# Twelve in place of eight weight pairs of a second feed-forward layer by seven products

## The chip, the cores and the metric

The kernel runs on one core of a Trainium2 chip. The metric is the device time of one execution in microseconds (us). Engines are called as in the profile: PE (TensorE matmul), PEld (its weight loads), DVE (VectorE), ACT (ScalarE), POOL (GpSimd), SP (SyncE, which issues all DMAs here).

## What is computed

```python
x = A_x                                   # 1 x 2048 x 576
xn = _layernorm(x, axis=-1)
return x + _A_ref(xn, A_wqkv, A_wo) + _B_ref(xn, B_w1, B_b1, B_w2)
# _A_ref: q, k, v = xn @ wqkv, 32 heads of 18; each position attends to 8 positions
#         (itself and every second one before it); softmax; o @ wo
# _B_ref: h = xn @ w1 + b1 (4608 wide); act = h * tanh(softplus(h)); act @ w2
```

All arithmetic is float32.

## The kernel before

**Float32 by halves.** A float32 operand is split into a high part (a cast, on ACT) and a low part (a difference, on DVE or POOL). One product is then three matmuls: high by high, low by high, high by low. A group of six matmuls over two contraction tiles of 128 fills one PSUM bank, and DVE adds that bank to an accumulator in SBUF (an eviction).

**Two halves, 18 pairs.** The 2048 tokens are two halves (`hf` 0 and 1) of 1024, each of two blocks `b` of 512. The 4608 hidden columns are 36 tiles of 128, taken as `NP = 18` pairs `q`. For each half: projections q/k/v (`qkv_item`, in the second half partly `z_part`), then `quad(hf, q)` for each pair, and at the end the output projection (`wo_part`). Within a pair, `m1_part` 0 to 5 computes both tiles of the first layer for both blocks with seven block products instead of eight (sums `Ss` of the activations, differences t0 and t1 of the weights).

**The second layer.** Ordinarily (`m2_pair` in half 0, `m2_cols` in half 1) one pair is four chunks (two blocks by two token groups), each of four banks of six matmuls 128x128 by 128x288. For pairs 0 to 7 of the second half the seven-product scheme is used: two pairs (`qq` 0 and 1) are one group `e`, whose seven items (`p_item`, products `P7, P4, P1, P5, P2, P6, P3`) have 24 matmuls each. The left factors are the activations `A11, A12, A22` and combinations `S1` to `S4` of them (`u_sum`; cast in `u_high`, low part in `u_low`); they are held in float32 until then, in buffers that `raw_act` hands out. The right factors are `B11, B21, B22` of the second layer's weight and the differences `T1` to `T4`. Each product has accumulators of its own, which POOL joins after the last group (`p_join`). Pair `2 * OC` is kept in float32 too and split afterwards (`a_split`). `OC` is the number of groups.

**The weights in DRAM.** Half 0 loads each weight, splits it (`make`), uses it and stores the split form (`keep`); half 1 loads that (`fetch`, `p_fetch`). For the pairs that go by seven products, half 0 also forms T1 to T4 (`t_sum`, `t_high`, `t_low`, `t_keep`, in the pool of tiles `xn`, five buffers) and stores each factor by itself. The second half reads pair `q + 1`'s weights as its pair `q` (`Q1`), so the pairs prepared in half 0 are 1 to `2 * OC`. Likewise differences of the q/k/v weights for `z_part` are prepared in half 0 (`z_load`, `z_sum`, `z_high`, `z_low`, `z_keep`, tiles from `xn`, for `k` = 0 and 1), and the output projection's in half 1 (`wo_load`, `wo_sum`, `wo_keep_high`, `wo_keep_low`, `wo_keep`; read back by `wo_fetch`).

**Order of the work.** Everything is written into a list `plan` of places. Each place holds one TensorE part (a projection item, an `m1_part`, a chunk or a product item); `before(i, fn)` puts side work ahead of place `i`. `spot(hf, q, i)` is place `i` of a pair. Each engine, and the SP queue, executes its own instructions strictly in that order. An ordinary pair has ten places (six parts and four chunks); an odd pair by seven products has nine (parts 0, 1, 2, item, 3, item, 4, item, 5), an even one ten (0, 1, item, 2, item, ...).

**Attention** is a generator (`attention(hf)`) of 73 steps a half, nine for two head groups: four of products q times k (POOL) with a reduction (DVE) one step later, one with the softmax's maximum, one with its sum and the first product with v, three more of those. The steps are dealt out over the plan: each place has a duration in plan units, multiplied by the `rate` of its stretch (`marks`), and the sum is divided into 146 equal shares.

```python
k = next(k for k in range(k + 1, len(plan)) if T[k + 1] > t and ok[k])
```

In half 0 only places 0, 3, 7 and 9 of a pair may take a step (`ok`); in half 1 the pairs by seven products may take them at all places.

Of the kernel before, what the change touches and what calls it, by code (L numbers as in the profile page):

```python
# [14 lines left out]
S, D, F = 2048, 576, 4608  # L15
# [11 lines left out]
NP = NF // 2  # L27
# [3 lines left out]
CU = 2 * DH  # L31
OC = 4
Q1 = [*range(1, NP), 0]
# [6 lines left out]
def block_kernel(ctx: ExitStack, tc: tile.TileContext, x, wq, wo, w1, b1, w2, mask, out):  # L40
# [1292 lines left out]
    def spot(hf, q, i):  # L1333
        return at["s", hf, q, i]

    for q in range(NP):
        if q == 0:
            i = at["q", 0, 3, 1, 0]
            ps_ = dict(raw=i - 3, sums=i - 1, wa=i, wc=i + 1, t0=i + 2, t1=i + 4)
        elif q == 1:  # L1340
            i = at["q", 0, 3, 0, 0]
# [16 lines left out]
    for q in range(1, 2 * OC + 1):  # L1358
        i = spot(0, q, (3,2)[q > 1])
# [12 lines left out]
    for name, k, d in (("T2", 0, 0), ("T2", 1, 1), ("T3", 0, 2), ("B11", 0, 3), ("B11", 1, 4), ("B21", 0, 5),  # L1372
                       ("B21", 1, 6), ("R2", 0, 7), ("T3", 1, 8), ("R3", 0, 9), ("T1", 0, 10), ("T1", 1, 10),
                       ("T4", 0, 11), ("T4", 1, 11), ("B22", 0, 11), ("B22", 1, 11)):
        before(i + d, lambda name=name, k=k: z_fetch(name, k))
    i = spot(0, 9, 4)
    for k in range(2):
        for n, steps in enumerate((
# [4 lines left out]
            for kind, name in steps:  # L1383
                f = dict(l=z_load, s=z_sum, h=z_high, o=z_low, k=z_keep)[kind]
                d = 30 + 2 * n if k else 2 * n if n < 10 else (19, 20, 22, 23, 25, 26, 27)[n - 10]
                before(i + d, lambda f=f, name=name, k=k: f(name, k))
# [64 lines left out]
    before(i + 6, var1)  # L1451
    i = spot(0, NP - 2, 0)
    for jj in range(JB):
# [23 lines left out]
    for q in range(2 * OC + 2):  # L1477
        for i in range(spot(1, q, 0), spot(1, q, 9) + 1):
# [3 lines left out]
             spot(1, 2, 0), spot(1, 2 * OC + 2, 0), spot(1, NP - 1, 0), at["o", 0, 0], at["o", 2, 0]]  # L1482
    rate = (1.15, 0.4, 0.5, 0.8, 1.15, 1.3, 1.2, 0.8, 1.5, 0.8, 0)
    T = [0.0]
# [17 lines left out]

    i = spot(1, *(11,3))
    for k in range(4):
        before(i - 8 + 2 * k, lambda k=k: wo_load(k))
    for n in range(4):
        before(i + (0,2,4,6)[n], lambda n=n: wo_sum(n))
    for n, name in enumerate(("T3", "T1", "T2", "T4", "B11", "B21", "B22", "R", "D")):
        k = i + 10 + (0,5,10,15,20,25,30,35,40)[n]
        if name == "R":  # L1510
            before(k - 8, lambda: wo_rest(0))
        before(k, lambda name=name, n=n: wo_keep_high(name, n))
        before(k + 1, lambda name=name: wo_keep_low(name))
        before(k + 2, lambda name=name: wo_keep(name))
# [69 lines left out]
```

## Time and profile before

| | us |
|---|---|
| median of 3 runs (lowest to highest) | 1123.72 (1123.23 to 1124.98) |
| span of the profiled execution | 1121.6 |
| PE busy | 1109.5 (99%) |
| DVE, POOL, ACT busy | 829.0, 787.7, 492.1 |
| DMA queue, share of 16 engines | 69.2% |

The profiled execution is shown by its span alone, from its first to its last instruction; no time of its own beyond that is given. Busy times of different engines overlap. The granted TensorE clock is 1.000 throughout. Which pair a time belongs to is read from the chain of work in order of time: an ordinary pair takes 24.1 us, pair 17 of the first half begins at 503.85, pair 2 of the second half at 652.96.

### The profile page before, as it was taken

The numbers are of one execution on the slowest core, as the hardware profiler recorded it, in microseconds if no ns is written. First come the engines' busy times: TensorE is split into PE (matmuls) and PEld (weight loads), VectorE is DVE, ScalarE is ACT, GpSimd is POOL, SyncE is SP. The second block draws the span as 40 slices with busy tenths as digits, with TensorE's granted clock in tenths as the row PEclk, the third lists the DMA queues.
The fourth block names the chain that finished last, engine by engine and source line by source line (L and its number), as shares of the span: only waits on it lengthen the run. The fifth ranks groups of instructions, "written<-read, shape, count | busy, mean of one in ns | idle before, by whom it ended". The sixth has DMA issues, their size and how long they took to land.

```text
span 1121.6 us, 18415 instructions
## 1 busy us (share of the span) xinstructions
PE 1109.5 (99%) x6630; PEld 1023.0 (91%) x6630; DVE 829.0 (74%) x1351; ACT 492.1 (44%) x892; POOL 787.7 (70%) x639
## 2 busy tenths in 40 slices
PE   8999999999999999999999999999999999999998
PEld 7999899999999999899999889999999999999998
DVE  6368788888888888877655456687866677776876
ACT  5544645544554545455233355343433343443332
POOL 2488767767689687676788476665789878668632
PEclk9999999999999999999999999999999999999999
DMA  6899885868767849666596797655655477676463
GB/s 200 283 312 318 290 283 205 289 228 284 261 240 258 282 163 345 222 240 214 191 342 238 231 373 249 241 200 174 227 198 189 168 263 269 215 253 248 157 222 104
DMA packets 147487, 271.08 MB, mean 242 GB/s; under 512 B 30114, under 2 KB 86724, under 8 KB 147396
## 3 DMA queue, kind: packets, MB, share of 16 engines
q1 hardware_dynamic: 147396, 269.91, 69.2%
q8 instruction: 52, 0.85, 0.3%
q14 instruction: 39, 0.32, 0.1%
HBM read 160.39 MB, written 109.48 MB: 241 GB/s over the span
## 4 chain that ended last, share of the span: by engine, by line
PE 89%; DVE 4%; POOL 3%; DMA 2%; issue 1%; ACT 1%; DVEq 0%; POOLq 0%; SPq 0%
PE h L657 28%; PE po L755 19%; PE pq L349 11%; PE po L868 10%; PE po L847 7%; PE h L663 5%; PE o L1056 4%; PE z L447 2%; DMA acc<-in_x 1%; POOL accP L856 1%; DVE u L801 1%; POOL pr L534 0%; DVE accP L871 0%; POOL act L709 0%; DMA z_B<-kept_wq 0%
## 5 line engine op out<-in xcount | busy, mean ns | idle before, releaser
L755 PEld LDWEIGHTS po<-w,act 128*128 128x128 f32 x1728 | 236.4, 188 | 7.5 <-DVE acc L759 1.7
L755 PE MATMUL po<-w,act 128*128 128x288 f32 x1728 | 240.8, 295 | 1.4 <-DVE acc L759 1.2
L534 POOL TENSOR_TENSOR pr<-q,kv 128x576 f32<-128x576 f32 x128 | 195.7, 1553 | 18.7 <-DMA q<-q_d 16.9
L572 POOL TENSOR_TENSOR pv<-L,kv 128x576 f32<-128x576 f32 x128 | 174.3, 1461 | 38.7 <-DVE L L565 20.9
L709 POOL TENSOR_TENSOR act<-c,act 128x512 fp32r<-128x512 f32 x81 | 107.1, 1322 | 128.4 <-ACT act L708 125.5
L759 DVE TENSOR_TENSOR acc<-po,acc 128x288 f32<-128x288 f32 x288 | 120.4, 450 | 31.6 <-PE po L755 30.2
L349 PE MATMUL pq<-wq,xt 128*128 128x432 f32 x672 | 136.2, 361 | 1.8 <-ACT xt L83 1.8
L868 PEld LDWEIGHTS po<-w,act 128*128 128x128 f32 x960 | 131.1, 188 | 3.7 <-DVE accP L871 0.4
L868 PE MATMUL po<-w,act 128*128 128x288 f32 x960 | 133.8, 295 | 0.2
L349 PEld LDWEIGHTS pq<-wq,xt 128*128 128x128 f32 x672 | 125.0, 188 | 8.7 <-ACT xt L83 2.7
L703 ACT ACTIVATE c<-c,b1c 128x512 f32<-128x512 f32 x81 | 58.7, 724 | 132.9 <-DVE c L702 132.6
L657 PE MATMUL h<-xt,t 128*128 128x512 f32 x432 | 110.6, 391 | 0.9 <-DVE c L702 0.8
L657 PE MATMUL h<-S,t 128*128 128x512 f32 x432 | 110.4, 391 | 0.0
L691 ACT COPY c<-h 128x512 f32<-128x512 f32 x81 | 47.4, 586 | 136.5 <-PE h L663 78.3
L578 DVE TENSOR_REDUCE og<-pv 128x144 f32<-128x1152 f32 x64 | 85.9, 1343 | 25.4 <-POOL pv L572 25.4
L657 PE MATMUL h<-xt,wa 128*128 128x512 f32 x432 | 104.0, 390 | 0.0
L657 PEld LDWEIGHTS h<-xt,wa 128*128 128x128 f32 x432 | 80.9, 188 | 16.9
L871 DVE TENSOR_TENSOR accP<-po,accP 128x288 f32<-128x288 f32 x160 | 69.6, 454 | 36.1 <-PE po L868 34.5
L847 PEld LDWEIGHTS po<-pw,u 128*128 128x128 f32 x672 | 92.4, 188 | 2.9 <-DVE u L801 0.5
L847 PE MATMUL po<-pw,u 128*128 128x288 f32 x672 | 94.2, 296 | 0.3 <-DVE u L801 0.3
L539 DVE TENSOR_REDUCE L<-pr 128x64 f32<-128x1152 f32 x64 | 85.8, 1341 | 11.2 <-POOL pr L534 11.1
L657 PEld LDWEIGHTS h<-xt,t 128*128 128x128 f32 x432 | 79.0, 188 | 16.1 <-DVE c L702 1.1
(231 smaller groups left out, 1840.5 us busy)
## 6 DMA issues: line engine op xcount, KB each, us to landing
kv<-kv_d SPq DMA_DIRECT2D x64, 396.0 KB, 5.2
kept_t<-t SPq DMA_DIRECT2D x36, 512.0 KB, 5.3
t<-kept_t SPq DMA_DIRECT2D x36, 512.0 KB, 5.4
rw<-in_w SPq DMA_DIRECT2D x36, 320.0 KB, 4.6
kept_wa<-wa SPq DMA_DIRECT2D x18, 640.0 KB, 3.5
kept_w<-w SPq DMA_DIRECT2D x20, 576.0 KB, 4.8
wa<-kept_wa SPq DMA_DIRECT2D x18, 640.0 KB, 6.1
w<-kept_w SPq DMA_DIRECT2D x20, 576.0 KB, 4.5
```

The source lines that it names most:

```text
L349: nc.tensor.matmul(pq[:, 0:432], XT[:, xi, tok], wt[wi][:, hl, 0:432], start=i == 0, stop=i == len(seq) - 1)
L534: nc.gpsimd.tensor_tensor(out=pr[:, x:x + hh], in0=q[:, j0 + x:j0 + x + hh, None, :].to_broadcast([P, hh, W, CU]), in1=win(kt, 0, CU, j0 + ...
L539: nc.vector.tensor_reduce(L[:, k, j0:j0 + hj].rearrange("p j w h -> p (j w h)"), pr.rearrange("p j w (h d) -> p (j w h) d", h=2), axis=AX, ...
L572: nc.gpsimd.tensor_tensor(out=pr[:, x:x + hj].rearrange("p j d w -> p j w d"), in0=L[:, k, x:x + hj, :, h:h + 1].to_broadcast([P, hj, W, DH]),
L578: nc.vector.tensor_reduce(og[:, :, c0:c0 + DH], pr, axis=AX, op=ALU.add)
L657: nc.tensor.matmul(ph, wt[:, wl, wk * P:(wk + 1) * P], X[:, xs, :], start=first and i == 0, stop=last and i == len(seq) - 1, skip_group_ch ...
L709: nc.gpsimd.tensor_tensor(out=a[:, 1, :], in0=t, in1=a[:, 0, :].bitcast(F32), op=ALU.subtract)
L755: nc.tensor.matmul(po, acts[hf, q, b, j][:, al, tok], done["w2", hf, 2 * q + j][:, wl, c * HC:(c + 1) * HC], start=i == 0, stop=i == 5)
L759: nc.vector.tensor_tensor(out=t, in0=po, in1=t, op=ALU.add)
L847: nc.tensor.matmul(po, units[e, k, qq][:, al, tok], w[:, qq, wl, :], start=i == 0, stop=i == 5)
L868: nc.tensor.matmul(po, acts[hf, q, b, j][:, al, tok], done["w2", hf, 2 * q + j][:, wl, c * HC:(c + 1) * HC], start=i == 0, stop=i == 5)
L871: nc.vector.tensor_tensor(out=t, in0=po, in1=t, op=ALU.add)
```

## The change

`OC` becomes 6: the second half's pairs 0 to 11 go by seven products, and the first half prepares T1 to T4 for pairs 1 to 12. The q/k/v differences begin in pair 12 at place 7 instead of pair 9 at place 4, one entry of their list a place. The loads of the second half's x for its layer norm in pair 16 begin two places later. Three of the eleven attention rates differ. The output weights' preparation begins at place 6 of pair 14 (was place 3 of pair 11), in another order and three places apart.

```diff
-OC = 4
+OC = 6
...
-    i = spot(0, 9, 4)
+    i = spot(0, 2 * OC, 7)
     for k in range(2):
         for n, steps in enumerate((
                 [("l", "B12"), ("l", "B22"), ("l", "B11")], [], [("s", "T3")], [("h", "T3")], [("o", "T3"), ("s", "T1")], [],
...
-                d = 30 + 2 * n if k else 2 * n if n < 10 else (19, 20, 22, 23, 25, 26, 27)[n - 10]
+                d = n + 19 * k
                 before(i + d, lambda f=f, name=name, k=k: f(name, k))
...
-    i = spot(0, NP - 2, 0)
+    i = spot(0, NP - 2, 2)
     for jj in range(JB):
         before(i + 2 * jj, lambda jj=jj: x_load(jj))
         before(i + 2 * jj + 6, lambda jj=jj: norm1(jj))
...
     marks = [at["q", 0, 2, 0, 1], at["q", 0, 3, 0, 0], spot(0, 1, 0), spot(0, 2 * OC + 1, 0), at["q", 1, 0, 0, 0], at["z", 0, 0], spot(1, 0, 0),
              spot(1, 2, 0), spot(1, 2 * OC + 2, 0), spot(1, NP - 1, 0), at["o", 0, 0], at["o", 2, 0]]
-    rate = (1.15, 0.4, 0.5, 0.8, 1.15, 1.3, 1.2, 0.8, 1.5, 0.8, 0)
+    rate = (1.15, 0.4, 0.55, 0.8, 1.15, 1.3, 1.2, 0.9, 1.3, 0.8, 0)
...
-    i = spot(1, *(11,3))
+    i = spot(1, 2 * OC + 2, 6)
     for k in range(4):
         before(i - 8 + 2 * k, lambda k=k: wo_load(k))
     for n in range(4):
         before(i + (0,2,4,6)[n], lambda n=n: wo_sum(n))
-    for n, name in enumerate(("T3", "T1", "T2", "T4", "B11", "B21", "B22", "R", "D")):
-        k = i + 10 + (0,5,10,15,20,25,30,35,40)[n]
+    for n, name in enumerate(("T3", "B11", "T2", "B21", "R", "T1", "T4", "B22", "D")):
+        k = i + 7 + 3 * n
         if name == "R":
             before(k - 8, lambda: wo_rest(0))
```

## The prediction

> **What bounds the kernel now.** I read the page first: busy shares and the chain that ended last.
>
> ```profile
> span 1121.6 us, 18415 instructions
> PE 1109.5 (99%) x6630; PEld 1023.0 (91%) x6630; DVE 829.0 (74%) x1351; ACT 492.1 (44%) x892; POOL 787.7 (70%) x639
> PE 89%; DVE 4%; POOL 3%; DMA 2%; issue 1%; ACT 1%; DVEq 0%; POOLq 0%; SPq 0%
> ```
>
> TensorE is busy in all but 12 us of 1121.6, and 89% of the chain is its matmuls. Next the view of waits, TensorE alone, for where it stood:
>
> ```profile
> PE pq L349 <- ACT xt L83: 1.8, 2, 1.1
> PE warm L67 <- POOL ident masks.py:199: 1.3, 1, 1.3
> PE o L1056 <- DVE y L1060: 1.3, 2, 0.7
> PE po L755 <- DVE acc L759: 1.2, 1, 1.2
> PE ta L77 <- ACT xn L182: 0.9, 1, 0.9
> PE h L657 <- DVE c L702: 0.8, 1, 0.8
> PE h L657 <- ACT rt L691: 0.7, 1, 0.7
> PE po L847 <- DVE u L801: 0.3, 1, 0.3
> ```
>
> Apart from the start (1.8 + 1.3 + 0.9) there are four places: 1.3 in the output stage, 1.2 in pair 15 of the first half, 0.8 in its pair 1, and 0.7 and 0.3 in the second half. So a matmul that is dropped comes off the span, unless a queue that was just in time becomes late. Then the windows by stage (columns: window and length, busy time of PE, PEld, DVE, ACT, POOL with instruction counts, clock, DMA share, GB/s), and two pieces of the chain in order of time:
>
> ```profile
> 333.53:357.61 24.08, 24.08 (x147) 22.09 (x147) 21.01 (x31) 11.17 (x20) 22.20 (x18) 1.00 0.62 207
> 607.77:631.80 24.03, 24.03 (x119) 22.49 (x120) 14.04 (x26) 5.66 (x18) 13.69 (x11) 1.00 0.31 92
> 677.77:722.95 45.18, 45.18 (x269) 41.10 (x269) 32.99 (x49) 18.09 (x32) 35.10 (x25) 1.00 0.66 229
> 722.95:768.71 45.76, 45.47 (x270) 41.15 (x269) 35.04 (x57) 19.88 (x31) 27.52 (x20) 1.00 0.61 207
> 848.00:896.27 48.27, 48.27 (x293) 44.19 (x293) 33.50 (x56) 16.09 (x24) 43.76 (x35) 1.00 0.57 207
> ```
>
> ```profile
> 683.67 3.17 PE po L847 x24
> 852.54 3.18 PE po L868 x24
> ```
>
> Two pairs by seven products take 45.18 us, two ordinary ones 48.27; both are all TensorE. One item or one chunk, 24 matmuls, takes 3.17 us (132.1 ns a matmul).
>
> **The change, part by part.** The sum is made against the profiled execution, span 1121.6; the median of the runs, 1123.72, is 2.1 above it, and I carry the difference over unchanged.
>
> *Matmuls.* Two more groups of two pairs: 2 x (8 chunks - 7 items) = 2 chunks less, 2 x 3.17 = **-6.34**. The two windows above say the same: 48.27 - 45.18 = 3.09 each. The Trainium skill, "TensorE: Matmul & The Clock Gate", section "Back-to-back issue gap", gives N / 2.4 + 2.5 ns for a warm matmul, for N = 288 an estimate of 122.5 ns; the gain by it would be 48 x 122.5 = 5.88 us. The row's 132.1 ns decides, and the page would make the forecast 0.46 us later.
>
> *Side work in the first half, pairs 9 to 12* (now like pairs 1 to 8), and in the second:
>
> ```profile
> L303 POOL TENSOR_TENSOR twT<-rw,twT 128x288 f32<-128x288 f32 x16 | 15.9, 997 | 1.3
> L313 DVE TENSOR_TENSOR twT<-twT,twhT 128x576 fp32r<-128x576 f32 x16 | 13.8, 894 | 0.3
> L308 ACT CAST twhT<-twT 128x576 fp32r<-128x576 f32 x16 | 10.8, 676 | 15.3 <-POOL twT L303 15.3
> L801 POOL TENSOR_TENSOR u<-ra,u 128x512 fp32r<-128x512 f32 x14 | 18.9, 1354 | 4.7 <-ACT u L795 4.5
> L801 DVE TENSOR_TENSOR u<-rm,u 128x512 fp32r<-128x512 f32 x12 | 11.8, 981 | 3.6 <-ACT u L795 3.6
> L795 ACT CAST u<-ra 128x512 fp32r<-128x512 f32 x22 | 13.5, 619 | 17.1 <-DVE ra L789 8.4 <-PE po L847 6.9 <-POOL ra L789 1.8
> L539 DVE TENSOR_REDUCE L<-pr 128x64 f32<-128x1152 f32 x64 | 85.8, 1341 | 11.2 <-POOL pr L534 11.1
> kept_w<-w SPq DMA_DIRECT2D x20, 576.0 KB, 4.8
> kept_T<-twhT SPq DMA_DIRECT2D x16, 288.0 KB, 4.8
> ```
>
> Per first-half pair: POOL 3 differences (3 x 0.997 = 3.0), DVE one difference and two low parts (taken at 1.0 too, + 2 x 0.894 = 2.8), ACT 2 x 0.676 = 1.4. SP issues 7 stores of 288 KB where it had 2 of 576: 864 KB more. Per second-half group: 14 unit casts for 8 (ACT +6 x 0.619 = 3.7), 14 low parts for 8 and 8 combinations, less 4 evictions: about +11 on DVE and POOL together; SP loads 7 x 576 KB for 4 x 576, three issues more. Cover: pairs 1 to 8 and groups 0 to 3 do just this now, and TensorE loses 0.8 + 0.3 us in all of them. I cost it at nothing by itself; without the cover the upper bound is the whole 2.8 of DVE a pair, 11.2 us. The SP queue has some 20 issues more in a stretch of 96 us; q/k/v differences used to be loaded and stored there and now come later.
>
> *Attention.* Its 146 steps are dealt out by plan time times `rate`. Worked through with the new OC and rates, the total falls from 894.1 to 821.2 plan units, so the steps move: first-half pairs 1 to 8 have 19 steps (were 15), 9 to 12 have 9 (were 13), 13 to 16 have 14 (were 12). In the second half pairs 2 to 13 have 45 (were 45), but pairs 0 and 1 have 7 of that half's own (were 2), and what is left after pair 17 is 2 steps (was 6). That last shift matters in the output stage, where these two reductions stood ahead of the evictions that TensorE waited for:
>
> ```profile
> 1056.52 1.34 DVE L578 TENSOR_REDUCE og<-pv 128x144 f32<-128x1152 f32 x1
> 1059.90 1.34 DVE L578 TENSOR_REDUCE og<-pv 128x144 f32<-128x1152 f32 x1
> ```
>
> Now the last step stands before the second of the four final chunks: **-1.3** (bounds -1.3 and 0). The first second-half steps load their k and q five plan places earlier, into the stretch with a DMA share of 0.31 (window 607.77), and no TensorE wait above is for them: 0.
>
> *The stall in pair 15.* A softmax step was followed in the next place by a value step, so DVE stood 2.40 us for POOL and its evictions came late:
>
> ```profile
> 458.56 1.35 DVE L578 TENSOR_REDUCE og<-pv 128x144 f32<-128x1152 f32 x1 [2.40 <-POOL pv L572]
> 463.90 1.54 DVE L759 TENSOR_TENSOR acc<-po,acc 128x288 f32<-128x288 f32 x4
> ```
>
> In the new plan these two steps are two places apart (14.7 and 14.9): **-1.2**. What comes in its place: the q/k/v differences, one list entry a place instead of every second, run from pair 12 place 7 to pair 16 place 2, beside 3 or 4 attention steps a pair. Pair 10 (window 333.53, 4 steps and the same differences at half the density) had POOL at 22.20 of 24.08 and no TensorE idle. One more difference of POOL a pair, 1 to 1.4 us, brings the four-step pairs 13 and 15 to some 23.5: full. Their loads also wait in the SP queue for tiles of the last stores of pair 12 (one landing, 4.8). Bounds 0 and 4 x 1.25; I take **+0.8**, nearer pair 10, which passed clean.
>
> *More steps in pairs 1 to 8.* In pair 1 a value step comes in at place 3, just ahead of the DVE chain behind the 0.8 wait; its reduction is 1.34, of which the chain has about 0.5 to spare (the idle time in the first row below): **+0.9** (0 to 1.34). In pair 3 the softmax step comes to place 3, with its reduction, 1.34, and what the three rows of such a step show:
>
> ```profile
> 126.56 0.69 DVE L257 TENSOR_TENSOR t<-tt,t 128x512 fp32r<-128x512 f32 x1 [0.51 <-ACT t L256]
> 188.91 1.00 DVE L549 TENSOR_TENSOR L<-L,mk 2x256 f32<-2x256 f32 x1
> 189.95 0.42 DVE L553 TENSOR_REDUCE m<-L 128x32 f32<-128x256 f32 x1
> 190.40 0.43 DVE L555 TENSOR_TENSOR L<-L,m 128x256 f32<-128x256 f32 x1
> ```
>
> 3.2 us together, ahead of four evictions: 0 to 3.2. I take **+0.8**, nearer the lower end, since in pairs 2 to 8 such steps pass now without a TensorE wait, though at places with less beside them.
>
> *Products of the second half.* An item writes four banks; evictions must be done before the next item comes round. At the first item of an odd pair they are nearly late:
>
> ```profile
> 728.80 1.36 DVE L801 TENSOR_TENSOR u<-ra_r,u 128x512 fp32r<-128x512 f32 x1 [1.82 <-ACT u L795]
> 730.08 1.77 DVE L789 TENSOR_TENSOR ra<-ra,ra_r 128x512 f32<-128x512 f32 x1
> 731.78 1.34 DVE L539 TENSOR_REDUCE L<-pr 128x64 f32<-128x1152 f32 x1
> 733.04 1.54 DVE L853 TENSOR_TENSOR accP<-po,accP 128x288 f32<-128x288 f32 x4
> 733.72 3.38 PE L847 MATMUL po<-pw,u 128*128 128x288 f32 x24
> ```
>
> The first of the four evictions ends near 733.49, and TensorE writes again at 733.72: a margin of about 0.2. Seven steps a group come where there were six (ten in the last, for eight), over six groups instead of four; at pair 11 place 3 it is a softmax step, 0.85 more than the plain reduction, so 0.6 late. Against 0.3 lost before, I take **+1.2** more (0 to 14 new items x 0.3 = 4.2).
>
> *Preparation of the output weights.* Four loads, four POOL sums and nine cast/low/store steps move from pair 11 to pairs 14 to 17, three places apart instead of five. Ordinary pairs there have DVE 33.5 of 48.27. Between the last one's store and the products that read it lie four chunks, 4 x 3.17 = 12.7 us: a store and a load of 4.8 each fit. SP holds its reload behind its store, and the attention loads behind that are few by then: 0, at most +1.
>
> Sum: -6.34 - 1.3 - 1.2 + 0.8 + 0.9 + 0.8 + 1.2 = -5.1. Profiled span 1116.5; time 1123.72 - 5.1 = **1118.6**.
>
> **Rivals.**
>
> *Nothing new stalls.* Every cover holds: -6.34 - 1.3 - 1.2 - 0.3 = -9.1, **1114.6**. For it: pairs 2 to 8 lost nothing. Against: the 0.2 margin.
>
> *Given back in pairs 13 to 16.* POOL is full, DVE waits for it in order as at 458.56, and each of the four pairs loses the 1.25 that pair 15 lost: +5.0 for the +0.8, **1122.8**. For it: POOL 22.20 with half the density. Against: that window's PE is 24.08 of 24.08. The Trainium skill, "SBUF — State Buffer", section "Who interferes with whom", has a DVE instruction with two SBUF inputs and a GpSimd one that reads SBUF exclude each other for a whole instruction, which speaks against the change, since nearly all that it adds is of these two kinds. The trace agrees in that L789 takes 1.77 at 730.08; it has no row in which this cost TensorE more than the waits above.
>
> *Slower.* In the products of the second half DVE is late as a rule: with the 0.2 margin gone, each item that gets one more reduction of 1.34 ahead of its evictions costs 1.1 us of TensorE. Without the term taken above the time is 1117.4; slower than 1125.97 needs 8 of the 42 items. At 12 it is 1117.4 + 13.2 = **1130.6**. Against: DVE is busy 35.04 of 45.76 with six steps, and one more adds 1.5.
>
> *The change doesn't drop the matmuls* can't be: their number follows from OC.
>
> **How the numbers follow.** About 0.2% (2.2 us) is what a measurement can tell: faster is below 1121.5, slower above 1126.0. Forecast 0.73, its own range 1115.5 to 1121.0; nothing new stalls 0.10; given back 0.12; slower 0.05. Faster 0.73 + 0.10 + 0.02 of the given-back case = 0.85; same 0.10; slower 0.05. The range 1115.2 to 1122.5 leaves out slower (0.05), most of the stall-free case (0.07) and half of given back (0.06).
>
> **What would show it.** L847 with 1008 matmuls for 672 and L868 with 576 for 960; two more two-pair windows near 45.2. No TensorE wait on L1060 early in the output stage and none in pair 15 at places 4 to 6; new ones on L702 in pair 1, L759 in pair 3 and in pairs 13 to 16, on L801 or L853 among the products. Wrong it would be if a wait names a DMA (the SP queue's part undercosted), or if the PE waits grow past 14 us in all.

## The result, and the profile after

| | before | after |
|---|---|---|
| median of 4 runs (lowest to highest), us | 1123.47 (1122.92 to 1124.98) | 1156.53 (1153.18 to 1160.01) |
| ratio | | 1.029 [1.0268, 1.0312] |
| span of the profiled execution | 1121.6 | 1158.2 |

Forecast was 1118.6, with a range up to 1122.5. The kernel became 33 us slower instead of 5 faster. The profiled execution of the changed kernel is the slowest of its four, so what is read from its trace adds up to 36.6 us. The page of the changed kernel: span, busy times, the clock in 40 slices, the chain by engine.

```profile
span 1158.2 us, 18408 instructions
PE 1119.3 (97%) x6582; PEld 1025.2 (89%) x6582; DVE 859.8 (74%) x1379; ACT 502.3 (43%) x913; POOL 812.4 (70%) x655
PEclk9999999999999999899998999999999998999999
PE 74%; POOL 11%; DVE 6%; issue 4%; ACT 2%; DMA 1%; SPq 0%; POOLq 0%; DVEq 0%; ACTq 0%
```

The 48 matmuls are gone (6582 for 6630), yet PE is busy 9.8 us longer. Span less PE busy is 38.9 us for 12.1. The busy shares of DVE and POOL did not rise at all: 74 and 70% before and after. Who TensorE waited for (total, times, longest):

```profile
PE h L657 <- DVE c L702: 7.8, 4, 3.8
PE h L657 <- DVE rt L702: 5.6, 3, 3.2
PE z L447 <- ACT zqs L456: 4.8, 2, 4.3
PE po L755 <- DVE acc L759: 4.5, 1, 4.5
PE po L847 <- DVE accP L853: 2.1, 2, 1.5
```

These twelve waits are 24.8 us: single stalls, not a broad slowing. The five longest in the timeline of TensorE (start, duration; in brackets the idle time before and its releaser):

```profile
131.82 2.86 PE L657 MATMUL h<-xt,t 128*128 128x512 f32 x6 [2.07 <-DVE c L702]
478.49 1.81 PE L755 MATMUL po<-w,act 128*128 128x288 f32 x6 [4.51 <-DVE acc L759]
621.20 2.53 PE L447 MATMUL z<-zraw_T,S 128*128 128x432 f32 x6 [4.33 <-ACT zqs L456]
769.02 1.94 PE L657 MATMUL h<-xt,t 128*128 128x512 f32 x6 [3.15 <-DVE rt L702]
969.68 2.93 PE L657 MATMUL h<-xt,t 128*128 128x512 f32 x6 [3.82 <-DVE c L702]
```

Six matmuls of L657 take 1.52 us otherwise; here 2.86 and 2.93 in two of the rows. Behind each of the five the granted clock fell to half. Windows over those stretches (window, length, busy PE, PEld, DVE, ACT, POOL, clock, DMA share, GB/s):

```profile
131.92:135.33 3.41, 3.41 (x8) 2.65 (x9) 3.41 (x6) 2.31 (x4) 2.86 (x3) 0.50 0.77 228
476.67:483.50 6.83, 5.01 (x21) 5.01 (x22) 5.03 (x10) 2.32 (x4) 3.94 (x4) 0.50 0.57 206
620.03:626.86 6.83, 5.66 (x16) 5.21 (x17) 3.33 (x7) 2.40 (x8) 3.88 (x4) 0.50 0.03 10
770.21:773.63 3.42, 3.42 (x13) 2.79 (x12) 3.42 (x4) 0.03 (x1) 3.31 (x3) 0.50 0.20 43
968.19:975.02 6.83, 5.33 (x16) 4.57 (x17) 4.76 (x11) 3.76 (x5) 3.29 (x4) 0.50 0.14 49
```

In these 27.3 us PE was busy 22.83, which full speed would have done in half: 11.4 us lost. The account against before is idle time +26.8, half clock +11.4, matmuls -6.3: 31.9 of the 36.6 us between the spans; the other 4.7 are in PE's busy time and are not assigned.

By stages, from the first matmul of a pair in each trace (after minus before): +5.8 at the start of pair 13 of the first half, +11.3 at pair 17, +21.5 at pair 2 of the second half, +33.3 at pair 8, +37.9 at pair 14, +38.3 at pair 17, +36.6 at the end. So the loss is 5.8 in pairs 1 to 12, 5.5 in 13 to 16 (all in 15), 10.2 in the q/k/v stage, 11.8 in pairs 2 to 7, 4.6 net in pairs 8 to 13, 0.4 in 14 to 16, and -1.7 at the end.

The 11.8 us of pairs 2 to 7 are mainly seven waits, 8.9 us together, and one half-clock window (1.7). Ahead of the longest of the waits (769.02 above) stand these two instructions of DVE:

```profile
767.03 1.34 DVE L539 TENSOR_REDUCE L<-pr 128x64 f32<-128x1152 f32 x1
768.29 0.68 DVE L702 TENSOR_TENSOR rt<-h,rt 128x512 f32<-128x512 f32 x1
```

The reduction of an attention step stands right ahead of the addition L702 that TensorE waits for. Before, at the same point of the work, it stood four us earlier (731.78, L702 at 735.69) and no wait followed.

### The profile page after: what moved, and what is told of

The parts are those of the page before. It is cut to its first block, busy times and chain, and to the rows that moved or that the text cites. A ratio compares the mean times of both kernels' runs of the same rounds, so it can differ in the third digit from the quotient of the medians.

```text
span 1158.2 us, 18408 instructions
## 1 busy us (share of the span) xinstructions
PE 1119.3 (97%) x6582; PEld 1025.2 (89%) x6582; DVE 859.8 (74%) x1379; ACT 502.3 (43%) x913; POOL 812.4 (70%) x655
## 4 chain that ended last, share of the span: by engine, by line
PE 74%; POOL 11%; DVE 6%; issue 4%; ACT 2%; DMA 1%; SPq 0%; POOLq 0%; DVEq 0%; ACTq 0%
PE h L657 23%; PE po L755 16%; PE po L847 9%; PE pq L349 8%; PE po L868 5%; PE o L1056 5%; PE h L663 4%; POOL pv L572 3%; PE z L447 2%; POOL pr L534 2%; POOL act L709 2%; POOL s L608 1%; DVE L L539 1%; POOL twT L303 1%; DVE w L257 1%
## 5 line engine op out<-in xcount | busy, mean ns | idle before, releaser
L755 PEld LDWEIGHTS po<-w,act 128*128 128x128 f32 x1728 | 238.8, 190 | 11.5 <-DVE acc L759 5.4
L755 PE MATMUL po<-w,act 128*128 128x288 f32 x1728 | 243.4, 297 | 4.7 <-DVE acc L759 4.5
L534 POOL TENSOR_TENSOR pr<-q,kv 128x576 f32<-128x576 f32 x128 | 199.8, 1586 | 21.0 <-DMA q<-q_d 21.0
L709 POOL TENSOR_TENSOR act<-c,act 128x512 fp32r<-128x512 f32 x69 | 92.4, 1339 | 106.0 <-ACT act L708 101.9
L847 PEld LDWEIGHTS po<-pw,u 128*128 128x128 f32 x1008 | 138.9, 189 | 10.8 <-DVE accP L853 3.4
L847 PE MATMUL po<-pw,u 128*128 128x288 f32 x1008 | 143.0, 297 | 4.4 <-DVE accP L853 2.1
L657 PE MATMUL h<-xt,t 128*128 128x512 f32 x432 | 114.2, 400 | 13.5 <-DVE c L702 7.8
L657 PE MATMUL h<-S,t 128*128 128x512 f32 x432 | 110.7, 391 | 0.7 <-ACT c L691 0.4
L578 DVE TENSOR_REDUCE og<-pv 128x144 f32<-128x1152 f32 x64 | 86.0, 1343 | 30.9 <-POOL pv L572 25.6
L657 PEld LDWEIGHTS h<-xt,t 128*128 128x128 f32 x432 | 80.4, 191 | 30.7 <-DVE c L702 9.1
L657 PE MATMUL h<-xt,wa 128*128 128x512 f32 x432 | 104.1, 390 | 0.0
L703 ACT ACTIVATE c<-c,b1c 128x512 f32<-128x512 f32 x69 | 50.0, 725 | 124.0 <-DVE c L702 123.6
L657 PEld LDWEIGHTS h<-xt,wa 128*128 128x128 f32 x432 | 80.9, 188 | 17.0
L657 PEld LDWEIGHTS h<-S,t 128*128 128x128 f32 x432 | 77.9, 188 | 14.3 <-ACT c L691 0.8
L868 PEld LDWEIGHTS po<-w,act 128*128 128x128 f32 x576 | 79.5, 190 | 4.5 <-POOL act L810 2.2
L868 PE MATMUL po<-w,act 128*128 128x288 f32 x576 | 81.1, 297 | 2.4 <-POOL act L810 2.0
L691 ACT COPY c<-h 128x512 f32<-128x512 f32 x69 | 40.5, 587 | 76.1 <-PE h L657 39.6
```

The lines of the kernel that those rows point to most:

```text
L534: nc.gpsimd.tensor_tensor(out=pr[:, x:x + hh], in0=q[:, j0 + x:j0 + x + hh, None, :].to_broadcast([P, hh, W, CU]), in1=win(kt, 0, CU, j0 + ...
L578: nc.vector.tensor_reduce(og[:, :, c0:c0 + DH], pr, axis=AX, op=ALU.add)
L657: nc.tensor.matmul(ph, wt[:, wl, wk * P:(wk + 1) * P], X[:, xs, :], start=first and i == 0, stop=last and i == len(seq) - 1, skip_group_ch ...
L709: nc.gpsimd.tensor_tensor(out=a[:, 1, :], in0=t, in1=a[:, 0, :].bitcast(F32), op=ALU.subtract)
L755: nc.tensor.matmul(po, acts[hf, q, b, j][:, al, tok], done["w2", hf, 2 * q + j][:, wl, c * HC:(c + 1) * HC], start=i == 0, stop=i == 5)
L847: nc.tensor.matmul(po, units[e, k, qq][:, al, tok], w[:, qq, wl, :], start=i == 0, stop=i == 5)
```

## The experiments

The expectations name theories. 'Steps' (later 'places', then 'queue order'): the loss comes from where the attention's steps stand among an engine's other instructions. 'Side work' (later 'load'): DVE and POOL have too much to do, wherever the steps stand, or the number of steps in a stage decides. 'q/k/v differences too dense': the denser preparation of these weights alone makes the loss. Wherever an edit says "steps", the loop that deals them out is replaced by a written list, and places are given as pair.place:

```diff
-        k = next(k for k in range(k + 1, len(plan)) if T[k + 1] > t and ok[k])
+    cuts = [21, 22, 24, ...]          # the 146 places
+    for n, k in enumerate(cuts):
```

**Which part of the change.** Four kernels, two of them mixtures of old and new.

*Old kernel, new steps.* Edit: steps at the changed kernel's places (second half up to pair 7; later, where the lists differ, spread alike).

> The kernel before (OC = 4, all its side work where it was) with its attention steps at the places that the changed kernel gives them (the same list up to pair 7 of the second half, 4 to 5 a pair after it). Theory 'steps': where the reductions and the products of the attention stand among the evictions is what costs; the first half and the projections after it lost 11 + 10 us in the changed kernel's trace, pairs 2 to 7 of the second half 12, so 1145 to 1157. Theory 'side work' (more differences, casts and low parts than DVE and POOL can take): 1123 to 1126. Theory 'q/k/v differences too dense': 1123 to 1126.

Measured 1149.78, ratio 1.023 [1.0182, 1.0277]. Most of the loss without a single matmul or weight difference of the change: +9.5 at pair 17, +19.7 at pair 2 of the second half, +30.6 at pair 8, the changed kernel's 11.3, 21.5 and 33.3 almost stall for stall; nothing after pair 8.

*New kernel, old steps.* Edit: the old places in the first half and up to pair 7 of the second; the 53 left over pairs 8 to 17 and after.

> The changed kernel with the attention steps at the places of the kernel before in the first half and up to pair 7 of the second; the 53 steps left are spread over pairs 8 to 17, four to six a pair, and six after them. Theory 'steps': 1115 to 1124, the two dropped chunks less (-6.3) and what the more crowded pairs 8 to 13 cost. Theory 'side work': 1145 or more, since all of it is still there. Theory 'q/k/v differences too dense': a stall of 4 us or more in pair 15 stays, 1123 to 1130.

Measured 1153.44, 1.0262 [1.0195, 1.0329]. That is the time 'side work' had named; the reverse does not hold. The q/k/v stage and pairs 2 to 7 are clean (+13.0, then +13.8), but there are four new stalls in pairs 9 to 12 of the first half (+8.7), the one in pair 15, and 11.3 net in pairs 8 to 13 of the second. "The new steps are bad" was too simple: each arrangement fails where it meets side work that it was not made for.

*New kernel, old steps in the second half alone.* Edit: the second half's list of the run before.

> The changed kernel with only the second half's steps as in the run before this one, the first half's as the change deals them. Theory 'steps': above that run by what the first half and the projections lost, 21 us: 1135 to 1146. Theory 'side work': within 4 us of that run. Theory 'q/k/v differences too dense': within 4 us of that run.

Measured 1158.91, 1.0311 [1.0281, 1.0341], 5.5 us above the run before: no theory had that. Pairs 2 to 7 lose nothing (+20.4 to +20.8), and pairs 8 to 13 lose it again (+32.9 at pair 14).

*Old kernel, new q/k/v preparation.*

```diff
-    i = spot(0, 9, 4)
+    i = spot(0, 12, 7)
...
+                d = n + 19 * k
...
-    i = spot(0, NP - 2, 0)
+    i = spot(0, NP - 2, 2)
```

> The kernel before with only the q/k/v differences (from pair 12 place 7, one entry a place) and the x loads of pair 16 moved as in the change. Theory 'steps': 1123 to 1127, since these differences alone only crowd POOL in pairs 13 to 16 where three steps a pair stand. Theory 'side work': 1123 to 1127. Theory 'q/k/v differences too dense': 1130 or more.

Measured 1128.96, 1.0039 [1.002, 1.0059], between the ranges of the theories: one stall, in pair 15, and two half-clock windows. DVE, POOL and PE there:

```profile
462.99 3.00 POOL L572 TENSOR_TENSOR pv<-L,kv 128x576 f32<-128x576 f32 x2
467.47 1.26 POOL L709 TENSOR_TENSOR act<-mn,act 128x512 fp32r<-128x512 f32 x1
468.69 1.26 POOL L709 TENSOR_TENSOR act<-c,act 128x512 fp32r<-128x512 f32 x1
469.91 1.09 POOL L395 TENSOR_TENSOR zB<-zB,zB 128x432 f32<-128x432 f32 x1
471.04 0.61 DVE L403 TENSOR_TENSOR zB<-zB,zhT 128x432 fp32r<-128x432 f32 x1 [6.27 <-POOL zB L395]
471.56 1.54 DVE L759 TENSOR_TENSOR acc<-po,acc 128x288 f32<-128x288 f32 x4
472.07 5.64 PE L755 MATMUL po<-w,act 128*128 128x288 f32 x24 [4.29 <-DVE acc L759]
```

Read from below: TensorE waits 4.29 us for four evictions that wait for nothing but DVE. DVE is idle, 6.27 us, because the instruction ahead of them in its queue wants a difference from POOL, and that stands behind an attention product, six short instructions of the layer norm and two activations. POOL is busy 17.16 of the 17.80 us before 471.00, so it is full here, though not over the whole pair (22.88 of 31.20). The stall comes of both: a full stretch of POOL, and a DVE instruction that waits for it right ahead of the evictions.

**Side work or steps.** Both kernels without the attention's arithmetic (its loads, stores and places stay, what it stores are zeros):

```diff
-                    for x in range(0, hj, hh):
-                        nc.gpsimd.tensor_tensor(
...
-                        nc.vector.tensor_reduce(
-                            L[:, k, j0:j0 + hj].rearrange("p j w h -> p (j w h)"),
...
-                        nc.vector.tensor_reduce(og[:, :, c0:c0 + DH], pr, axis=AX, op=ALU.add)
...
+                            nc.vector.memset(og, 0.0)
```

> The kernel before with the arithmetic of the attention left out (products, reductions and softmax of all 146 steps; its loads, its stores and the steps' places stay; what it stores are zeros). Both theories: TensorE's matmuls stay, its waits outside the start nearly go, 1118 to 1122 (1123.7 less the 1.2 + 0.8 + 0.7 + 0.3 of waits in the FFN at most).

> The changed kernel with the same left out. Theory 'places': the two added groups and the q/k/v preparation in its new place cost nothing by themselves; the kernel is 6.3 us (48 matmuls of 132.1 ns) below the kernel before without attention, 5 to 8 with the measurement's noise: 1111 to 1116. Theory 'load': the added side work costs even alone; less than 3 us of gain, 1116 to 1125.

Measured 1118.62 (0.9957 [0.9941, 0.9974]) and 1111.58 (0.9895 [0.988, 0.9909]): 7.0 us apart. First lines of the two pages, old and new:

```profile
span 1116.7 us, 17971 instructions
PE 1107.6 (99%) x6630; PEld 1022.7 (92%) x6630; DVE 600.8 (54%) x1151; ACT 454.7 (41%) x851; POOL 421.1 (38%) x383
```

```profile
span 1109.7 us, 17937 instructions
PE 1101.5 (99%) x6582; PEld 1016.5 (92%) x6582; DVE 628.0 (57%) x1179; ACT 464.8 (42%) x871; POOL 442.2 (40%) x399
```

Alone, the change is what it was meant to be: PE is at 99% in both, and pair 14 of the second half starts at 934.7 for 941.0, 6.3 us earlier. Weight differences, unit work, dense q/k/v and output weights cost nothing by themselves. The loss is between them and the attention. Both kernels lack the attention's load as well as its order, so they do not tell these two apart. They also set a floor: the old kernel with attention is 4.9 us of span above its own, the changed one 48.5.

**One step.** Old kernel, a single step moved:

```diff
-    cuts = [..., 40, 49, 51, ...]      # 1.7
+    cuts = [..., 40, 45, 51, ...]      # 1.3
```

> The kernel before, with one of its 146 attention steps moved by four list places: the last value step of the first unit group stands at place 3 of pair 1 in place of place 7, where the changed kernel has it. Theory 'queue order' (the POOL product of that step, about 3.3 us, stands ahead of POOL's last weight difference; ACT's cast, DVE's low part and, behind it in DVE's queue, the addition L702 come late, so TensorE waits): the wait in pair 1 goes from 0.85 to about 2.1 us, and with the half clock of one 3.41 us window after it (1.7 lost) the kernel is 2.9 to 3.8 us slower: 1126.4 to 1127.6, nothing changed elsewhere. Theory 'load' (only the number of steps in a stage matters): no change, within 0.5 us of the kernel before.

Measured 1126.19, 1.002 [1.0012, 1.0029]; in the trace +3.1 us between pairs 0 and 2, 0.9 in pair 2 of the second half, and nothing else. The wait is as expected (0.85 to 2.07 us), the time just below its range of 1126.4 to 1127.6; the mechanism is simpler than I wrote. In this pair the step's reduction (L578) itself stands in DVE's queue ahead of the evictions, and the addition L702 starts at 130.79 where it started at 129.54:

```profile
124.24 1.34 DVE L578 TENSOR_REDUCE og<-pv 128x144 f32<-128x1152 f32 x1
...
130.79 0.68 DVE L702 TENSOR_TENSOR c<-h,c 128x512 f32<-128x512 f32 x1
131.52 1.65 PE L657 MATMUL h<-xt,t 128*128 128x512 f32 x6 [2.07 <-DVE c L702]
```

Three windows one behind the other show the price of that wait:

```profile
129.59:133.00 3.41, 1.48 (x7) 1.24 (x8) 3.41 (x7) 1.47 (x3) 2.78 (x4) 1.00 0.97 305
133.00:136.42 3.42, 3.42 (x14) 3.23 (x13) 3.31 (x4) 1.41 (x3) 1.73 (x1) 0.50 0.89 297
136.42:139.83 3.41, 3.41 (x23) 3.10 (x22) 2.39 (x4) 0.91 (x2) 2.40 (x2) 1.00 1.07 391
```

PE is idle 1.93 of the first window's 3.41 us, and in the whole next one it has 14 matmuls where it then has 23. So 1.22 us of added wait cost another 1.71.

**The same number of steps, shifted.** Old kernel, the steps from pair 17 through the q/k/v stage one to eight places earlier (the expectation says one to four): 19 in that stage as before, five in pair 17 for three, none in pair 0 of the second half for two.

> The kernel before, with the attention steps of the first half's last pair and of the q/k/v stage of the second half at the changed kernel's places: still 19 steps in that stage, each one to four places earlier. Theory 'queue order': the softmax steps come onto ACT and DVE just ahead of the copies that the z matmuls wait for; the 10.2 us which that stage lost in the changed kernel (0.45 + 1.54 + 4.33 of waits and 6.83 us at half clock) come back here, 8 to 12, with up to 2 us more in pair 17, where two steps more stand: 1131 to 1137. Theory 'load': the same number of steps in the stage, 0 to 2 us, 1123 to 1126.

Measured 1134.76, 1.0094 [1.0078, 1.0109]: +10.4 in that stage. Its main stall, on three engines:

```profile
605.77 1.35 DVE L539 TENSOR_REDUCE L<-pr 128x64 f32<-128x1152 f32 x1 [1.33 <-POOL pr L534]
608.97 0.92 DVE L555 TENSOR_TENSOR L<-L,m 128x256 f32<-128x256 f32 x1
609.93 0.42 ACT L559 ACTIVATE L<-L 128x256 f32<-128x256 f32 x1 [4.85 <-DVE L L555]
610.53 0.28 ACT L456 COPY zqs<-z 128x144 f32<-128x144 f32 x1
610.86 2.53 PE L447 MATMUL z<-zraw_T,S 128*128 128x432 f32 x6 [4.39 <-ACT zqs L456]
```

ACT has the softmax's exponential next and waits 4.85 us for DVE's side of it; the 0.28 us copy that frees TensorE's bank stands behind. This settles number against place for this stage: same number, 10 us.

**Placing by hand, first tries.** Changed kernel, first half: steps off place 3 where a stall was, old places from pair 17 through the q/k/v stage; then the second half too (none at the end of the products).

> The changed kernel, with only the attention steps of the first half put elsewhere: of pairs 1 to 16 every step that stood at list place 3 just ahead of a late eviction goes one or two places on (1.3 to 1.7, 5.3 to 5.7, 11.3 to 11.7, 15.3 to 15.7), with at most one step more or less in a pair, and from pair 17 through the z stage the old places, with the same 19 steps there. Number of steps in the half unchanged; second half untouched. Theory 'places' (a loss is one reduction that waits for POOL in order, right ahead of an eviction; how many steps a stage holds matters little): the losses before the second half, 3.8 in pair 1, 1.6 in pair 5, 0.9 in pair 11, 5.4 in pair 15 and 10.2 in the z stage, fall from 21.5 to 0 to 6 (pair 15 may keep up to 5.5, which the denser q/k/v preparation costs alone), and the time is 1136 to 1141 for 1156.5. Theory 'load' (POOL and DVE have too much to do with two more groups, wherever the steps stand): 15 or more of the 21.5 stay, time 1150 to 1157.

> As the run before, and the second half's attention steps put elsewhere too: in pairs 1 to 4 the old places of the list, 11 steps for 14; pairs 5 to 12 as in the changed kernel; none between place 5 of pair 12 and place 8 of pair 13, where the joins of the products stand; 5 to 6 steps in pairs 14 to 17, six after them. Theory 'places': beyond the run before, the 12.4 us of pairs 1 to 4 and the 10.9 at the end of the products go, with 0 to 6 us of new losses in the fuller pairs 14 to 17: 1115 to 1123. Theory 'load': the loss moves to pairs 14 to 17, and no more than 8 us are gained on the run before.

Measured 1147.0, 1.0213 [1.0188, 1.0238], and 1150.07, 1.0241 [1.0218, 1.0263]. The q/k/v stage lost nothing, pairs 1 and 5 were clean, and pairs 6, 8, 9 and 14 stalled in their stead (+9.8 at pair 13). 13.8 us were lost before the second half, between the 0 to 6 of 'places' and the 15 or more of 'load': a step moved out of one collision went into the next. In the second, pairs 8 to 13 lose 2.5 for 10.9 (+21.0 to +17.2, 6.3 of it the matmuls'), but pairs 14 to 16 lose 13.7 (+30.9 at pair 17), as 'load' had it; nothing was gained on the first. Pair 8 of the first shows the chain that I had expected in pair 1:

```profile
304.09 3.35 POOL L572 TENSOR_TENSOR pv<-L,kv 128x576 f32<-128x576 f32 x2
307.27 0.79 POOL L303 TENSOR_TENSOR twT<-rw,twT 128x288 f32<-128x288 f32 x1
308.10 0.67 ACT L308 CAST twhT<-twT 128x576 fp32r<-128x576 f32 x1 [4.13 <-POOL twT L303]
308.80 0.76 DVE L313 TENSOR_TENSOR twT<-twT,twhT 128x576 fp32r<-128x576 f32 x1 [2.58 <-ACT twhT L308]
309.48 0.68 DVE L702 TENSOR_TENSOR c<-h,c 128x512 f32<-128x512 f32 x1
310.22 1.65 PE L657 MATMUL h<-xt,t 128*128 128x512 f32 x6 [2.56 <-DVE c L702]
```

A 3.35 us product ahead of one 0.79 us difference goes through ACT and twice through DVE into 2.56 us of TensorE. The next arrangement therefore has no step at place 3 in pairs 1 to 11.

**Placing by hand, by rules.** First half: only places 0, 7 and 9 in pairs 1 to 11. Second half: old places in pairs 2 to 7, the old order of kinds at the end of the products. Then the places that still stalled were changed (the two lists for pairs 1 to 12 of the first half):

```diff
-1.7 1.9 2.7 2.9 3.7 3.9 4.0 4.7 4.9 ... 8.0 8.7 8.9 ... 12.0 12.3 12.7 12.9
+0.5 1.7 1.9 2.7 2.9 3.3 3.7 3.9 4.7 4.9 ... 7.3 7.7 7.9 8.7 8.9 ... 11.3 11.7 11.9 12.7 12.9
```

> The changed kernel, its 146 steps put by hand where the runs so far showed no stall: in pairs 1 to 12 of the first half only places 0, 7 and 9 (a product of POOL at place 3 stands ahead of the last weight difference), never a value step at place 0 right behind one at place 9; the old places from pair 17 on and in the z stage; in the second half the old places in pairs 2 to 7, the same phase at the end of the products as the old kernel had at the end of its own (the softmax step at place 7 of the last but one pair), 5 to 7 steps in pairs 14 to 17, six after them. Theory 'queue order': what is left are single new stalls of 1 to 4 us, mostly in pairs 13 to 16 of the first half (5.4 lost now) and 14 to 17 of the second; 1115 to 1127, the middle near 1121. Theory 'load': as much as in the other arrangements with these weights comes up elsewhere, 1140 or more.

> As the run before (all steps of the changed kernel placed by hand, 1131.8), with the places at which it still stalled changed: in pairs 4, 8 and 12 of the first half no second softmax step at place 0 right behind the first one at place 9 (that lost 1.8, 4.0 and 1.4 us there); the softmax step, which puts no product on POOL, stands at place 3 of pairs 3, 7 and 11 in its stead. In the second half the third step of pair 1 goes to pair 6, and one step each of pairs 16 and 17 goes to pairs 14 and 0. Theory 'queue order': the 7.2 us of the first half fall to 0 to 2, the 1.3 us after pair 1 go, some 2 of the 6 us in pairs 15 to 17 go: 1121 to 1126, the middle 1123.5. Theory 'load': the loss comes up in other pairs, 1130 or more. Whether the arrangement ends below the kernel before (1124) is open.

Measured 1131.79, 1.0067 [1.0053, 1.008], and 1130.97, 1.006 [1.0047, 1.0074]. The first takes 25 us off the changed kernel by nothing but the list, below the 1140 that 'load' asked for, but above the 1127 of 'queue order'. In the second the first half is done (+0.2 at its pair 17), but 3.8 us came up where a step was added in pair 0 of the second half (and the first half's last four were drawn together), and 6.2 where one was added at 14.1, so its time missed 'queue order' and lies in the range of 'load'.

Next, both of those back, and the one step that is over at 14.0, at 8.8 or at 15.2:

> The changed kernel with its steps as in the second arrangement by hand for the first half (0.2 us lost there against the kernel before), pairs 0, 1 and 17 of the second half back at the places without a stall, and the one step that is then over at place 0 of pair 14, one place behind the last step of pair 13. Theory 'queue order': the 3.8 us after pair 0 and the 6.2 around pair 14 of the second arrangement go, 0 to 3 come back behind the step at pair 14 place 0; 1121 to 1125. Theory 'load' (with two more groups there is no room for 146 steps): 1128 or more.

> As the run before, but the one step that is over stands at place 8 of pair 8 of the second half, so that every later step up to pair 13 is the next one of its kind (the softmax step at pair 12 place 4 in place of place 7). Theory 'queue order': the count is the same in pairs 14 to 17 and one more in pair 8; only the order of kinds at the end of the products differs: a stall of 2 to 10 us there, as the changed kernel had 10.9 with its own order, or none: 1121 to 1132. Theory 'load': 1128 or more.

> As the two runs before, but the step that is over stands at place 2 of pair 15, where the output weights are prepared: six steps in that pair and in pair 16. Theory 'queue order': 0 to 4 us lost in pair 15 (17 lost 4.0 with a step at place 2): 1120 to 1126. Theory 'load': 1128 or more.

Measured 1132.06 (1.0074 [1.0062, 1.0086]), 1130.08 (1.0048 [1.0036, 1.006]) and 1130.69 (1.0069 [1.0055, 1.0083]): all three in the range that was named for 'load', the second in that of 'queue order' too. At pair 14 of the second half they stand at -3.3, -2.7 and -2.8 against the old kernel; the whole loss is in pairs 14 to 16, to +8.8, +6.8 and +6.5 at pair 17. There the output weights are prepared.

**The output weights.** The 8.8 arrangement, with their work spread out:

```diff
-        before(i - 8 + 2 * k, lambda k=k: wo_load(k))
+        before(i - 8 + k, lambda k=k: wo_load(k))
-        before(i + (0,2,4,6)[n], lambda n=n: wo_sum(n))
+        before(i - 2 + n, lambda n=n: wo_sum(n))
-        k = i + 7 + 3 * n
+        k = i + 3 + (0, 3, 7, 10, 14, 17, 21, 24, 28)[n]
```

> As the run with the step in pair 8 (1130.1; against the two kernels without attention it has lost 0.7 us at the start of pair 14 and 9.5 more in pairs 15 to 17), with the preparation of the output weights spread out: its four loads a place apart, its four sums a place apart and four places earlier, its nine cast, low part and store steps three or four places apart from pair 14 place 9 on in place of three from pair 15 place 3 on. Theory A, the dense preparation among five to six steps a pair makes the stalls of pairs 15 to 17 (DVE's low parts L957 and the evictions behind them wait for POOL in order): at least 4 of the 9.5 go, 1121 to 1126. Theory B, the steps alone make them: within 2 us of 1130.

Measured 1126.41, 1.0031 [1.0019, 1.0043]: +1.8 at pair 17 for +6.8. Theory A, 0.4 above its upper edge; the density of this preparation beside four to six steps a pair cost some 5 us. At the turn of pair 15, where TensorE still lost 0.90 + 0.82 and a half-clock window, the rows of POOL and DVE are odd:

```profile
960.89 1.50 POOL L999 TENSOR_TENSOR raw_T<-rB,rB 128x576 f32<-128x576 f32 x1
962.28 1.49 POOL L856 TENSOR_TENSOR accP<-accP,accP 128x576 f32<-128x576 f32 x1
963.68 1.48 POOL L999 TENSOR_TENSOR raw_T<-rB,raw_T 128x576 f32<-128x576 f32 x1
965.06 1.35 POOL L709 TENSOR_TENSOR act<-c,act 128x512 fp32r<-128x512 f32 x1
966.31 1.49 POOL L999 TENSOR_TENSOR raw_T<-rB,raw_T 128x576 f32<-128x576 f32 x1
962.88 5.20 DVE L555 TENSOR_TENSOR L<-L,m 128x256 f32<-128x256 f32 x1
```

A subtraction that takes 0.42 us elsewhere takes 5.20: it starts while POOL is at work, and ends at 968.08, 0.28 after POOL's fifth instruction.

Last, the sums two places apart (`i - 3 + 2 * n`), and then one step of pair 4 from 4.3 to 4.6 and the next from 4.6 to 4.8:

> As the run with the output weights spread (1126.4), with their four sums two places apart in place of one. In that run POOL did four sums and joins in a row at the start of pair 15, and one subtraction of DVE's softmax beside them took 5.20 us where it takes 0.42 elsewhere; TensorE then lost 0.90 + 0.82 and one half-clock window (1.7). Theory 'queue order': the sums no longer stand in a row, the 3.4 us go: 1122 to 1124.5. Rival, the steps leave no room: they come back in pairs 15 to 17, 1126 to 1129.

> As the run before, and in pair 4 of the second half the second softmax step goes from place 3 to 6 and the value step from 6 to 8: there a value product on POOL stood ahead of two low parts L801, DVE's L789 waited for them 3.85 us, and TensorE 1.75 for the eviction behind. Theory 'queue order': another 1.8 to 3 us less, 1120 to 1122.5, below the kernel before (1123.4 in the runs before). Rival: a stall of the same size at the new place, 1122 to 1126.

Measured 1126.12 (1.0019 [1.001, 1.0028]) and 1123.82 (1.0006 [0.9998, 1.0015]). The sums gained nothing in time, as the rival had it: four instructions in a row were left on POOL, L555 still took 3.81 us, and 1.96 us of wait came at the next chunk. The step in pair 4 took its stall away as expected (-2.2 in the trace, +0.7 for +2.9 at pair 8), but the time lies above the 1122.5 of 'queue order'. The last arrangement equals the old kernel:

```profile
span 1123.6 us, 18422 instructions
PE 1107.2 (99%) x6582; PEld 1017.4 (91%) x6582; DVE 854.8 (76%) x1379; ACT 502.8 (45%) x912; POOL 814.6 (72%) x655
```

Nothing in the work differs from the changed kernel's but the list of steps and when the output weights are prepared: 33 us. No arrangement tried is below the old kernel; at pair 14 the last one is 4.5 ahead of it and loses 5.3 in pairs 14 to 16. The number of steps is not what differs there: pairs 14 to 17 have 4, 5, 6 and 5 with six after them, the old kernel five each and six after them. The output weights beside them are prepared three to four places apart for five, and other kinds of steps stand at other places. Which of the two it is, and whether a better list exists, is open.

## Why the prediction was wrong

- *Matmuls, -6.34*: right (6.3 at pair 14 and 7.0 in time, without the attention).
- *Side work at nothing by itself*: right, in those same two kernels. "By itself" was the trouble. Its cover left out the 0.7 in pair 0 of the second half.
- *Attention tail, -1.3*: right; no wait on L1060 is left after.
- *Pair 1, +0.9 (0 to 1.34)*: the step of the working is right, the wait grew by 1.22. What it lacked is the clock, 1.71 more.
- *Pair 15, -1.2 + 0.8 (0 to 5)*: the place was right, and the reason (POOL full, DVE waiting for it in order), the size not: a wait of 4.51 and two windows at half clock. The old kernel with that preparation alone lost 5.5 there. "Nearer pair 10, which passed clean" was the error. The rival "given back" had the mechanism; that its +5.0 is close to the 5.5 is luck, since it spread it over four pairs.
- *Pair 3, +0.8*: nothing there; 1.27 in pair 5 and 0.60 in pair 11 instead.
- *Products, +1.2, and the first attention steps of the second half earlier, 0*: here the sum broke. Pairs 2 to 7 lost 11.8, which the old `OC` shows too with the new steps. The rival "slower" had the place and the reduction ahead of what TensorE waits for (767.03), and with 1130.6 the nearest time; I gave it 0.05.
- *The q/k/v stage*: no term at all, 10.2 lost. It has 19 steps before and after.
- *The end of the products*: no term of its own; about 11 lost in pairs 8 to 13, against the 6.3 that the matmuls gave there.
- *Output weights, 0 to +1*: right for the changed kernel (0.4 from pair 14 to 17). With the steps by hand, 15 in pairs 14 to 16 for 14, 9.5 were lost beside the same preparation, and spreading it took some 5 of them back. Why the changed kernel lost nothing there is not shown.

The step that failed: I counted steps by pair and stage ("pairs 2 to 13 have 45 (were 45)") and let the count set the price, nothing for the q/k/v stage and 1.2 us for the products of the second half. The runs showed 10.2 in the first, 11.8 in pairs 2 to 7 and about 11 in pairs 8 to 13. What counted in its place is which step stands ahead of which instruction that TensorE waits for: at an equal count, other places cost the old kernel 10.4 us in the q/k/v stage, and one step moved by four places cost it 3.1 in pair 1. Load has a part where POOL is full for a stretch, as in pair 15; elsewhere its part was not separated. The sign of being wrong that the prediction named, waits that grow past 14 us, came: idle time grew by 26.8. The second omission is the clock. Its row stood at 1.000 in the profile before, so I took a wait at its own length; here 1.9 us of it cost 1.7 more.

The Trainium skill, "TensorE: Matmul & The Clock Gate", section "What's actually happening", has a free-running window of 3413 ns and half clock after at least one idle window. The trace agrees on the window (changes of the clock on a grid of 3.41 us), and not on the idle: 1.92 us, less than a whole window, was enough.

## What to carry to other kernels

When a change shifts a hand-made order, list for each moved instruction what stands directly behind it on its engine and how late that may be; equal counts and unchanged busy shares did not show the loss here (74% and 70% before and after). Look for stretches in which a side engine runs without a pause, too: its share over a whole pair hides them. Test it by moving one step in the old kernel, and take the neighbour's work away in both kernels to see what the change is worth alone. In a kernel that keeps TensorE at 99%, price each wait of about 2 us with the half-clock window that may follow it.

## What the runs showed of the hardware

- *Half clock after partial idle.* All changes of the granted clock in these traces lie on a grid of 3.41 us, whose start differs from run to run. Idle time of TensorE within one such window (gaps over 0.25 us) was followed by half clock in the next from 1.92 us on in each of 32 cases; between 1.72 and 1.90 it went either way; at 1.71 or less never (windows at full clock, all traces here, without the start). One gap can therefore cost one or two windows, by where the grid lies: 4.39 us cost one in the old kernel with its q/k/v steps shifted, 4.29 us two with its new q/k/v preparation. The same wait may also cost none: of the eleven runs of the old kernel with one step moved, four had a mean granted clock of 1.000 (1124.45 to 1126.05 us) and seven 0.998 or 0.999 (1126.18 to 1127.75 us).
- *DVE shut out by POOL.* A DVE subtraction of 0.42 us (L555) lasted 5.20 beside five POOL instructions in a row (it began in the second) and 3.81 beside four, ending 0.28 us behind POOL's last. The Trainium skill, "SBUF — State Buffer", section "Who interferes with whom", has the port pair that DVE shares with GpSimd as an exclusive lock; the trace agrees: of the 288 instances of L555 in the traces with attention, 39 took over 0.6 us, and each of them ended 0.28 or 0.29 us behind the end of a POOL instruction. In eight of these DVE got no turn between two or more POOL instructions in a row. That is no rule: one other did get it, and 65 that began in the last 0.2 us of a POOL instruction, with the next one right behind, took 0.42 to 0.48 us.
- *No price of placement is stable.* Place 3 was clean in pairs 2, 3 and 8 of the changed kernel, and in the first try by hand TensorE waited 2.56 us behind it in pair 8, with a value step there both times.
